# Moving the tanh of a feed-forward gate between the exps of attention's forward slots

## The chip, the cores and the metric

One core of a Trainium2 chip runs the whole program. The metric is the device time of one execution in microseconds (us); runs of one kernel agree within some tenths of a per cent. The engines have separate instruction queues, each worked off in order: PE (matrix multiplication; its weight loads are shown as PEld), DVE (vector), ACT (activations), POOL (GpSimd) and SP (issues most DMAs). They wait for each other by semaphores.

## What is computed

Forward and backward of a transformer block in parallel form, for one sequence of 2048 tokens of width 448, 16 heads of width 28, a feed-forward width of 1792:

```
xn  = layernorm(x)
out = x + attention(xn; wqkv, wo) + (silu(xn @ w_gate) * (xn @ w_up)) @ w_down
returned: out, and the gradients of x, wqkv, wo, w_gate, w_up, w_down for a given grad_out
```

Inputs and outputs are bf16. silu(a) is built from a tanh: with t = tanh(a / 2), silu(a) = a (1 + t) / 2, and the gradient of silu needs t too.

## The kernel before

The kernel has a forward stage and a backward stage, and the order of all instructions is written out by hand. The edit is in the forward stage.

**Slots.** Attention's scores and exponentials are cut into 256 slots: 4 groups of 4 heads, 4 chunks of 512 queries, 16 tiles of 128 keys. The function `slot(i)` issues, in this order:

- four score matmuls on PE (L625), one for each head, that run side by side in rows of 32. The first two write the tile `s_w`, which has one buffer of two PSUM banks; the other two write one bank each of `s_ps`, which has three buffers for two tiles in each slot. So the first two of a slot wait for the wide exp of the slot before, and the fourth waits for the first single exp of the slot before;
- three exps on ACT: a wide one over both banks of `s_w` (L628, 128x1024) and two single ones over the `s_ps` banks (L630, 128x512 each). They write `eT` tiles, which `o_unit` multiplies with the values (L467) once four slots are complete;
- filler work, by `fill.pump(FWD_NS, i)`. The class `Fillers` holds a list of units, written as generators that issue a matmul and yield its assumed cost in ns. In each slot it issues units until their costs reach a budget of 1740 ns. Attention's own later steps (`o_unit`, `mid1` to `mid3`, `dwo_unit`) are put first, and then a fixed stream, `items`.

**The stream.** For each of the 14 chunks of the feed-forward width (`fc`) and 4 token chunks (`sc`), 56 pairs in all, there are an `a_unit` (gate projection, L380), a `u_unit` (up projection, L404) and a `dh_unit` (gradient of the hidden layer, L418), two rounds apart: a round is a(i), then the gate work of i-1 with u(i-2), then dh(i-2). Between them stand weight-gradient units `dw_unit` (L437, 16 matmuls that read `f_sp`, the DMA transpose of a pair's results `hda`, issued on SP) and the qkv projections of the next head group (L292). Units take PSUM banks `gen` in turn.

**The tanh.** After its four matmuls an `a_unit` copies the result from PSUM with DVE (`ag`, L385) and issues the tanh on ACT (`tt`, L386), within the filler work of its slot; so on ACT's queue it stands behind the second single exp of that slot and ahead of the wide exp of the next one. `gate_ops` (L394 on DVE, L395 to L397 on POOL) reads `tt` and `ag` a round later, and `u_unit` and `dh_unit` read what it leaves (L410, L411, L423, L424). `tt` has two buffers, `ag` three.

The forward ends with the last slot and the end of the stream; `turn_loads` then issues the loads of the backward's first operands on SP (L742 to L747). The backward (from L763 on) is not touched.

Of the kernel before, what the change touches and what calls it, by code (L numbers as in the profile page):

```python
# [8 lines left out]
ACT = mybir.ActivationFunctionType  # L9
# [96 lines left out]
def kernel(  # L106
# [23 lines left out]
    PE, DVE, ACTE, POOL, SP = nc.tensor, nc.vector, nc.scalar, nc.gpsimd, nc.sync  # L130
# [63 lines left out]
    def new_gen(shape, dtype, name):  # L194
        return fill.bank().tile(shape, dtype, name=name)
# [156 lines left out]
    def load_fw(fc):  # L352
        w = ff.tile([P, 3, DP_], BF16, name="w_f")
        wT = ff.tile([P, 3, 4, P], BF16, name="wT_f", bufs=3)
        w4 = w[:].rearrange("p a (c f) -> p a c f", c=4)
        POOL.memset(w4[64:, 0:2, 3, :], 0.0)
        POOL.memset(w[:, 2, D:], 0.0)
        fsl = slice(fc * P, (fc + 1) * P)
        for a, src in ((0, B_w_gate), (1, B_w_up)):
            POOL.dma_start(out=w4[:, a, 0:3, :], in_=src[0:384, fsl].rearrange("(c p) f -> p c f", p=P))  # L360
            POOL.dma_start(out=w4[:64, a, 3, :], in_=src[384:448, fsl])
        POOL.dma_start(out=w[:, 2, :D], in_=B_w_down[fsl, :])
        fw[fc] = (w4[:, 0], w4[:, 1], wT[:, 2], lambda: sp_transpose(
            wT[:].rearrange("p a c d -> p (a c) d"), w[:].rearrange("p a n -> p (a n)"),
            (wT_d[:, fc], wT[:, 0:2].rearrange("p a c d -> p a (c d)"))))
        if fc > 0:
            fw_T(fc)
# [6 lines left out]
    def a_unit(fc, sc):  # L374
        if sc == 2 and fc + 1 < NFC:
            load_fw(fc + 1)
        ssl = slice(sc * 512, (sc + 1) * 512)
        ps = new_gen([P, 512], FP32, name="gen")
        for c in range(4):
            PE.matmul(ps[:], lhsT=fw[fc][0][:, c, :], rhs=xnT[:, c, ssl], start=(c == 0), stop=(c == 3))  # L380
            if c < 3:
                yield 216
        ag = ff.tile([P, 512], FP32, name="ag", bufs=3)
        tt = ff.tile([P, 512], FP32, name="tt")
        DVE.tensor_copy(out=ag[:], in_=ps[:])  # L385
        ACTE.activation(out=tt[:], in_=ag[:], func=ACT.Tanh, scale=0.5)  # L386
        ffs[fc, sc] = [ag, tt]
        yield 216

    def gate_ops(fc, sc):  # L390

        ag, tt = ffs[fc, sc]
        nn = ff.tile([P, 512], FP32, name="nn")
        DVE.scalar_tensor_tensor(out=ag[:], in0=tt[:], scalar=1.0, in1=ag[:], op0=ALU.add, op1=ALU.mult)  # L394
        POOL.tensor_scalar(out=nn[:], in0=tt[:], scalar1=-0.5, scalar2=0.5, op0=ALU.mult, op1=ALU.add)  # L395
        POOL.tensor_tensor(out=nn[:], in0=nn[:], in1=ag[:], op=ALU.mult)  # L396
        POOL.tensor_tensor(out=nn[:], in0=nn[:], in1=tt[:], op=ALU.add)  # L397
        ffs[fc, sc].append(nn)
# [63 lines left out]
    def o_unit(g, qc, m, eTs):  # L462
        ps = new_gen([P, 512], FP32, name="gen")
        for kt in range(4 * m, 4 * m + 4):
            for hh in range(4):
                r = HP * pv(hh)
                PE.matmul(ps[r:r + HP, :], lhsT=VS[g][:, kt, r:r + HP], rhs=eTs[kt][hh // 2][:, hh % 2, :],  # L467
                          start=(kt % 4 == 0), stop=(kt % 4 == 3), tile_position=(0, r), skip_group_check=True)
            if kt % 4 < 3:
                yield 216  # L470
        if m == 0:
            oacc[g, qc] = wk.tile([P, 512], FP32, name="oacc")
            DVE.tensor_copy(out=oacc[g, qc][:], in_=ps[:])
        else:
            DVE.tensor_tensor(out=oacc[g, qc][:], in0=ps[:], in1=oacc[g, qc][:], op=ALU.add)
        o_done.add((g, qc, m))
        yield 316

    def mid1(g, qc):
        acc = oacc.pop((g, qc))  # L480
        ps = new_gen([P, 4, P], FP32, name="gen")
        for qi in range(4):
            PE.transpose(ps[:, qi, :], acc[:, qi * P:(qi + 1) * P], ident_f[:])
            if qi < 3:
                yield 260
        o4 = ps[:].rearrange("p q (h r) -> p q h r", r=HP)
        rl = wk.tile([P, 4, 4], FP32, name="rl")
        DVE.reciprocal(out=rl[:], in_=o4[:, :, :, 28])
        t = wk.tile([P, 2, 4, P], BF16, name="od", bufs=5)
        DVE.tensor_tensor(out=t[:, 0].rearrange("p q (h r) -> p (q h) r", r=HP),  # L490
                          in0=ps[:].rearrange("p q (h r) -> p (q h) r", r=HP),
                          in1=rl[:].rearrange("p q h -> p (q h)").unsqueeze(2).to_broadcast([P, 16, HP]),
                          op=ALU.mult)
        od[g, qc] = (t, rl)
        yield 260

    def mid2(g, qc):
        t, rl = od[g, qc]
        ps = new_gen([P, 4, P], FP32, name="gen")
        for qi in range(4):  # L500
            for c in range(4):
                tok = (qc * 4 + qi) * P
                PE.matmul(ps[:, qi, :], lhsT=dyT[:, c, tok:tok + P], rhs=woT[:, c, g * P:(g + 1) * P],
                          start=(c == 0), stop=(c == 3))
                if qi * 4 + c < 15:
                    yield 60
        p3 = ps[:].rearrange("p q (h r) -> p (q h) r", r=HP)
        rl1 = rl[:].rearrange("p q h -> p (q h)")
        prod = wk.tile([P, 16, HP], FP32, name="prod", bufs=1)
        DVE.tensor_tensor(out=prod[:], in0=p3, in1=rl1.unsqueeze(2).to_broadcast([P, 16, HP]), op=ALU.mult)  # L510
        late_q.append((t, prod, rl1))
        yield 60
# [23 lines left out]
    def dwo_unit(g):  # L536
        ps = new_gen([P, 512], FP32, name="gen")
        for t in range(NT):
            PE.matmul(ps[:, :D], lhsT=od[g, t // 4][0][:, 0, t % 4, :], rhs=dy_sp[:, t, :],
                      start=(t == 0), stop=(t == NT - 1))  # L540
            if t < NT - 1:
                yield 189
        o = wk.tile([P, D], BF16, name="dw_o", bufs=1)
        DVE.tensor_copy(out=o[:], in_=ps[:, :D])  # L544
        for hh in range(4):
            h = g * 4 + hh
            (POOL if g == G - 1 else SP).dma_start(out=out_3[h * DH:(h + 1) * DH, :], in_=o[HP * pv(hh):HP * pv(hh) + DH, :])
        yield 189
# [10 lines left out]
    def ug(b, j):  # L559
        if j < len(chain):  # L560
            gate_ops(*chain[j])
        yield from u_unit(*b)
# [47 lines left out]
    def once(u):  # L610
        next(u)
        yield 0

    def slot(i):
        nonlocal eTs
        g, qc, kt = i // 64, (i // 16) % 4, i % 16
        qsl = slice(qc * 512, (qc + 1) * 512)
        m = i - EB // 2
        if m >= 0 and m % 4 == 0:
            fill.until(lambda: (m // 64, (m // 16) % 4, (m % 16) // 4) in o_done, i)  # L620
        wide = ps_w.tile([P, 2, 512], FP32, name="s_w")
        sp4 = [wide[:, 0], wide[:, 1]] + [ps_s.tile([P, 512], FP32, name="s_ps")[:] for _ in range(2)]
        for hh in range(4):
            r = HP * hh
            PE.matmul(sp4[hh], lhsT=KK[g][r:r + HP, kt * P:(kt + 1) * P], rhs=QQ[g][r:r + HP, qsl],  # L625
                      start=True, stop=True, tile_position=(r, 0))
        e2 = [wk.tile([P, 2, 512], BF16, name="eT", bufs=EB) for _ in range(2)]
        ACTE.activation(out=e2[0][:], in_=wide[:], func=ACT.Exp, scale=SCALE)  # L628
        for j in range(2):
            ACTE.activation(out=e2[1][:, j], in_=sp4[2 + j], func=ACT.Exp, scale=SCALE)  # L630
        eTs[kt] = e2
        if kt % 4 == 3:
            fill.first.append((i + 1, lambda e=dict(eTs): o_unit(g, qc, kt // 4, e)))
        if kt == 15:
            fill.first.append((i + 3, lambda: mid1(g, qc)))
            fill.first.append((i + 4, lambda: mid2(g, qc)))
            m3 = mid3(g, qc)
            fill.first.append((i + 5, lambda: once(m3)))
            fill.first.append((i + 6, lambda: once(m3)))
            fill.first.append((i + 7, lambda: once(m3)))  # L640
            if qc == 3:
                fill.first.append((i + 6, lambda: dwo_unit(g)))
            eTs = {}
        fill.pump(FWD_NS, i)
# [25 lines left out]
    for t in range(4):  # L670
        run(T_unit(xnT, xn_t, t, t % 2 == 0, ps_s if t < 2 else None))
    DVE.tensor_reduce(out=r_ones[:],
                      in_=ident_f[:].rearrange("p (a b) -> p a b", b=HP)[:, :, 28:30],
# [771 lines left out]
```

## Time and profile before

| | us |
|---|---|
| median of 3 runs | 1437.01 (1435.54 to 1440.87) |
| span of the profiled execution | 1438.2 |
| its forward slots with tanhs in them: scores of slot 14 to scores of the last slot | 53.3 to 608.1 |
| first backward score matmul | 616.3 |

The profiled execution has no time of its own beside its span, from the first instruction to the last; the span is 1.2 us over the median of the runs.

A row of a group of instructions reads: line of the kernel, engine, operation, tiles written <- tiles read, shapes, count | busy us, mean ns of one | idle us of the engine just before them, and which instruction ended that idle time. A row of the waits reads: who waited <- for whom: total us, times, longest. A row of the timeline reads: start, duration, engine, line, operation, and in brackets the idle time before it and what ended it. PEclk is the clock that PE was granted, as a share of full speed. Matmuls are pipelined and their ends are modelled, so PE's busy time can hold waits.

### The profile page before, as it was taken

The numbers are of one execution on the slowest core, as the hardware profiler recorded it, in microseconds if no ns is written. First come the engines' busy times: TensorE is split into PE (matmuls) and PEld (weight loads), VectorE is DVE, ScalarE is ACT, GpSimd is POOL, SyncE is SP. The second block draws the span as 40 slices with busy tenths as digits, with TensorE's granted clock in tenths as the row PEclk, the third lists the DMA queues.
The fourth block names the chain that finished last, engine by engine and source line by source line (L and its number), as shares of the span: only waits on it lengthen the run. The fifth ranks groups of instructions, "written<-read, shape, count | busy, mean of one in ns | idle before, by whom it ended". The sixth has DMA issues, their size and how long they took to land. (4 is left out here: it accounts for less than half of the span.)

```text
span 1438.2 us, 34638 instructions
## 1 busy us (share of the span) xinstructions
PE 1321.2 (92%) x12625; PEld 539.0 (37%) x12686; DVE 1154.8 (80%) x2001; ACT 1264.2 (88%) x2190; POOL 411.8 (29%) x577
## 2 busy tenths in 40 slices
PE   5899999989999999989999989999999999999995
PEld 2333333333333333333343434433443334443333
DVE  6677757656666676578999989888899999999988
ACT  4799988989889998869999989999989999899974
POOL 6574514454434454211121211201111112020005
PEclk9999999999999999989999999999999999999998
DMA  5796957796578676699999999999999999999981
GB/s 154 183 205 160 237 116 169 179 190 157 149 164 191 153 155 153 176 243 233 219 213 227 206 227 173 221 219 223 223 169 200 200 216 218 212 186 207 190 142 60
DMA packets 681116, 270.22 MB, mean 188 GB/s; under 512 B 607338, under 2 KB 655970, under 8 KB 680946
## 3 DMA queue, kind: packets, MB, share of 16 engines
q1 hardware_dynamic: 672498, 254.78, 87.1%
q0 software_dynamic: 7040, 12.93, 4.1%
q8 instruction: 99, 1.62, 0.5%
q14 instruction: 71, 0.58, 0.1%
q10 hardware_dynamic: 1408, 0.30, 0.1%
HBM read 64.37 MB, written 59.62 MB: 86 GB/s over the span
## 5 line engine op out<-in xcount | busy, mean ns | idle before, releaser
L864 DVE TENSOR_TENSOR ds_sb<-db,e_sb 128x512 bf16<-128x512 f32 x1024 | 646.5, 685 | 48.6 <-issue 22.4
L858 ACT ACTIVATE e_sb<-sb 128x512 bf16<-128x512 f32 x1024 | 555.0, 611 | 53.7 <-PE db L842 37.1
L628 ACT ACTIVATE eT<-s_w 128x1024 bf16<-128x1024 f32 x256 | 263.8, 1030 | 47.0 <-PE s_ps L625 43.8
L630 ACT ACTIVATE eT<-s_ps 128x512 bf16<-128x512 f32 x512 | 280.2, 611 | 0.0
L842 PE MATMUL db<-kd,qd 32*128 32x512 bf16 x1024 | 238.0, 385 | 8.6 <-DVE ds_sb L864 7.5
L834 PE MATMUL sb<-kd,qd 32*128 32x512 bf16 x1024 | 210.9, 389 | 5.3 <-DMA qd<-QD_d 3.4
L983 POOL TENSOR_TENSOR dq_acc<-dq_acc,dq_st 128x256 f32<-128x256 f32 x64 | 46.4, 724 | 497.7 <-ACT dq_st L981 497.7
L941 PE MATMUL acc<-ds_sb,qd 128*32 128x512 bf16 x1024 | 161.3, 391 | 0.0
L937 PE MATMUL acc<-e_sb,qd 128*32 128x512 bf16 x1024 | 159.2, 392 | 1.3 <-DVE dw_o L544 1.3
L924 ACT COPY dsT<-db 128x1024 bf16<-128x1024 bf16 x128 | 130.0, 1016 | 18.4 <-PE db L919 17.3
L396 POOL TENSOR_TENSOR nn<-nn,ag 128x512 f32<-128x512 f32 x56 | 71.3, 1274 | 249.7 <-DVE ag L394 241.1
L625 PE MATMUL s_ps<-QQ,KK 32*128 32x512 bf16 x512 | 126.2, 385 | 4.1
L1149 PE MATMUL genb<-wguT,dau_c 128*128 128x448 bf16 x448 | 117.5, 355 | 6.3 <-ACT dq_st L981 3.9
L625 PE MATMUL s_w<-QQ,KK 32*128 32x512 bf16 x512 | 100.2, 387 | 12.8 <-ACT eT L628 9.8
L834 PEld LDWEIGHTS <-qd 32*128 32x128 bf16 x1024 | 48.2, 91 | 146.3 <-issue 136.9
L437 PE MATMUL gen<-xn_t,f_sp 128*128 128x448 bf16 x416 | 91.8, 354 | 2.6 <-DVE nn L411 1.7
L437 PEld LDWEIGHTS <-f_sp 128*128 128x128 bf16 x640 | 55.7, 98 | 76.7 <-issue 31.6
L919 PE MATMUL db<-ident_bf,ds_sb 128*128 128x128 bf16 x1032 | 80.3, 222 | 0.9 <-DVE ds_sb L864 0.9
L968 PE MATMUL genb<-dsT,kd 128*32 128x256 bf16 x2048 | 79.2, 274 | 1.1
L919 PEld LDWEIGHTS <-ds_sb 128*128 128x128 bf16 x1032 | 69.1, 99 | 23.6 <-issue 5.1
L397 POOL TENSOR_TENSOR nn<-nn,tt 128x512 f32<-128x512 f32 x56 | 72.1, 1287 | 4.4
L625 PEld LDWEIGHTS <-KK 32*128 32x128 bf16 x1024 | 29.1, 91 | 115.3 <-issue 112.5
(179 smaller groups left out, 1951.7 us busy)
## 6 DMA issues: line engine op xcount, KB each, us to landing
F_d<-hda SPq DMA_DIRECT2D x56, 384.0 KB
dau_c<-F_d SPq DMA_DIRECT2D x24, 512.0 KB
qd<-QD_d SPq DMA_DIRECT2D x16, 512.0 KB
kd<-KD_d SPq DMA_DIRECT2D x16, 384.0 KB
dsT<-ds_sb SPq DMA_TRANSPOSE x383
h_c<-F_d SPq DMA_DIRECT2D x8, 512.0 KB
wT_d<-wT_f SPq DMA_DIRECT2D x14, 256.0 KB
KD_d<-qk_sp SPq DMA_DIRECT2D x7, 512.0 KB
```

The costliest lines, as they stand in the source:

```text
L437: PE.matmul(ps[:, :D], lhsT=fsp[fc][:, t // 4, w, t % 4, :], rhs=rhs[:, t, :], start=(t == 0), stop=(t == NT - 1))
L625: PE.matmul(sp4[hh], lhsT=KK[g][r:r + HP, kt * P:(kt + 1) * P], rhs=QQ[g][r:r + HP, qsl], start=True, stop=True, tile_position=(r, 0))
L628: ACTE.activation(out=e2[0][:], in_=wide[:], func=ACT.Exp, scale=SCALE)
L630: ACTE.activation(out=e2[1][:, j], in_=sp4[2 + j], func=ACT.Exp, scale=SCALE)
L834: PE.matmul(s_ps[:], lhsT=qside[g, qc][r:r + HP, 0, qi * P:(qi + 1) * P], rhs=kside[g, kc][r:r + HP, 0, :], start=True, stop=True, tile_po ...
L842: PE.matmul(d_ps[:], lhsT=qside[g, qc][r:r + HP, 1, qi * P:(qi + 1) * P], rhs=kside[g, kc][r:r + HP, 1, :], start=True, stop=True, tile_po ...
L858: ACTE.activation(out=est[k][:, j], in_=sps.pop((k, j))[:], func=ACT.Exp, scale=SCALE)
L864: DVE.tensor_tensor(out=ds[:, j], in0=dps.pop((k - 1, j))[:], in1=est[k - 1][:, j], op=ALU.mult)
L919: PE.transpose(ps[:, c, :], ds[:, c // 4, (c % 4) * P:(c % 4 + 1) * P], ident_bf[:])
L924: ACTE.copy(out=o, in_=ps[:])
L937: PE.matmul(a[r:r + HP, :], lhsT=sp4[:, 1, r:r + HP], rhs=e[:, j, :], start=first, stop=last, tile_position=(0, r), skip_group_check=True)
L941: PE.matmul(a[r:r + HP, :], lhsT=sp4[:, 0, r:r + HP], rhs=ds[:, j, :], start=first, stop=last, tile_position=(0, r), skip_group_check=True)
```

## The change

The `a_unit` no longer issues the tanh, but puts it on a list. `slot` issues what is on the list between its two single exps. `gate_ops` first issues its own pair's tanh, should that still be on the list.

```diff
@@ a_unit
         DVE.tensor_copy(out=ag[:], in_=ps[:])
-        ACTE.activation(out=tt[:], in_=ag[:], func=ACT.Tanh, scale=0.5)
+        tanhs.append((fc, sc, tt, ag))
         ffs[fc, sc] = [ag, tt]
         yield 216
 
+    tanhs = []
+
+    def tanh_flush(*only):
+        for x in list(tanhs):
+            if not only or x[:2] == only:
+                tanhs.remove(x)
+                ACTE.activation(out=x[2][:], in_=x[3][:], func=ACT.Tanh, scale=0.5)
+
     def gate_ops(fc, sc):
-
+        tanh_flush(fc, sc)
         ag, tt = ffs[fc, sc]
@@ slot
         for j in range(2):
             ACTE.activation(out=e2[1][:, j], in_=sp4[2 + j], func=ACT.Exp, scale=SCALE)
+            if j == 0:
+                tanh_flush()
         eTs[kt] = e2
```

On ACT's queue the order around a tanh was: single, single, **tanh**, wide, single, single. It becomes: single, single, wide, single, **tanh**, single.

## The prediction

> **What bounds the kernel now.** The edit touches one activation of the forward stage, so I read the page's engine rows, then the groups of ScalarE (ACT), the waits, and single slots of the timeline. The page (engine, busy us, share of the span, instructions):
>
> ```profile
> PE 1321.2 (92%) x12625; PEld 539.0 (37%) x12686; DVE 1154.8 (80%) x2001; ACT 1264.2 (88%) x2190; POOL 411.8 (29%) x577
> ```
>
> PE and ACT are both near full, but a mean over stages does not say who waits. The tanhs run from 54.1 to 578.7 us, within the forward slots (start of slot 14 at 53.3, last scores at 608.1). Groups of ACT, whole span (count | busy, mean ns | idle before, by whom):
>
> ```profile
> L628 ACT ACTIVATE eT<-s_w 128x1024 bf16<-128x1024 f32 x256 | 263.8, 1030 | 47.0 <-PE s_ps L625 43.8
> L386 ACT ACTIVATE tt<-ag 128x512 f32<-128x512 f32 x56 | 35.8, 640 | 18.5 <-DVE ag L385 13.2 <-POOL nn L397 2.3 <-DVE dl L525 1.4
> L340 ACT ACT_TABLE_LOAD x1 | 1.3, 1283 | 3.5 <-issue 3.5
> ```
>
> ACT has 47.0 us of idle time waiting for scores: in the forward it is mostly PE that sets the pace. But in 18.5 us it stands before a tanh whose input is not there, with the next wide exp queued behind it. Does PE pay for that? The waits between 56 and 611 us (total, times, longest):
>
> ```profile
> ACT eT L628 <- PE s_ps L625: 32.2, 71, 3.9
> ...
> ACT tt L386 <- DVE ag L385: 12.5, 22, 1.5
> ...
> PE s_w L625 <- ACT eT L628: 9.8, 20, 2.3
> ```
>
> PE waits 9.8 us openly. The timeline of slot 122 (start, us, ..., idle before) shows that this is not all:
>
> ```profile
> 300.50 0.39 PE L625 MATMUL s_w<-QQ,KK 32*128 32x512 bf16 x2
> ...
> 300.73 0.68 DVE L385 COPY ag<-gen 128x512 f32<-128x512 f32 x1
> ...
> 301.51 0.63 ACT L386 ACTIVATE tt<-ag 128x512 f32<-128x512 f32 x1 [0.82 <-DVE ag L385]
> ...
> 302.05 1.01 ACT L628 ACTIVATE eT<-s_w 128x1024 bf16<-128x1024 f32 x1
> ...
> 302.95 1.08 ACT L630 ACTIVATE eT<-s_ps 128x512 bf16<-128x512 f32 x2
> ...
> 303.10 0.39 PE L625 MATMUL s_w<-QQ,KK 32*128 32x512 bf16 x2 [0.40 <-ACT eT L628]
> ...
> 303.11 0.85 PE L625 MATMUL s_ps<-QQ,KK 32*128 32x512 bf16 x2
> ```
>
> In an undisturbed slot the wide exp starts 0.49 us after the scores; here 302.05 - 300.50 = 1.55, as the tanh waited for its copy until 301.51. The next scores then wait 0.40 us for the one wide bank. Their last two matmuls take 0.85 instead of 0.39: the fourth, in the third s_ps bank, waits another 0.46 us for the first single exp, and all later PE work with it. That counts as busy. So this slot lost 0.40 + 0.46 = 0.86 us of PE.
>
> **The change part by part.** It removes and adds no instruction, DMA or buffer. 56 tanhs of 0.64 us move past one wide and one single exp of the next slot on ACT's queue; nothing moves on SP's or POOL's. Two slots of 56 may differ: the gate work of the first pairs comes so soon that it flushes its tanh itself.
>
> Step 1, the waits before the tanh go. In its new place a tanh starts at the earliest 0.49 + 0.90 + 0.48 = 1.87 us after its slot's scores (exp starts 0.90 apart after a wide one, 0.48 after a single one). Its copy is done by 1.63 us at the latest in every slot (the trace's copy ends against the scores), so it waits no more; only the third tanh has another wait, POOL's until 59.1 us, and there the wide exp has passed before it. The ceiling is the 18.5 us.
>
> Step 2, what of that reaches PE. Slot 122 again: wide at 300.99, single 301.89, tanh 302.37, last single 302.91, ACT free at 303.39. Scores of slot 123 come at 302.70 without a wait; their wide exp would start at 303.19 and starts at 303.39, 0.20 late; its first single ends at 303.39 + 0.90 + 0.61 = 304.90 and lets the fourth matmul of slot 124 go at 304.95. PE fills 2.11 us between, so slot 124 starts at 304.81, and that matmul is 0.14 late. Lost: 0.14 in place of 0.86. I did the same sum for all slots from 14 to 255, with the filler time of PE as it ran, a wide exp 1.00 + 0.05 before the next scores, a single one 0.61 + 0.05 before the fourth matmul, and 0.54 us of ACT for a tanh. For the order of before it puts the last scores at 607.6 (read: 608.05), with 38.3 us lost on PE behind ACT; for the new order 21.7; without any tanh 14.6. So tanhs cost 23.7 us of PE now and 7.1 after: **-16.6 us**, all of it from the 31 tanhs with over 60 ns of idle before them. Moving the 25 others alone comes to +0.6 or nothing: a ready tanh delays the next wide exp as much from one place as from the other.
>
> Step 3, what is late next. PE also waits for DVE and DMA in the forward, some 19 us. Where DVE is behind (nine places, waits of 0.2 to 1.3 us), PE gets there earlier and waits longer, by at most what was gained since DVE last stood idle. Summed over them that gives **+3.2 us**.
>
> Step 4, what comes later than before. Behind the tanh now stands the second single exp, 0.54 us later. Its readers are the o units' last matmuls, and only in slots whose index is 3 mod 4, some 14 tanhs. Such an exp then ends about 3.0 us after its scores, the matmul comes 2.16 + 1.0 after them: covered by 0.1 on the median, short by as much in quick slots. Bounds 0 and 14 x 0.2 = 2.8; I take **+1.0**, near the median. The gate work L394 (DVE) and L395 (POOL) reads the tanh: from the trace, tanh ends in the new place come before their starts in all but the first two slots, by 0.23 us at the least; no cost, or 0.5 us of DVE each if those few slip, and DVE has 33% idle time there.
>
> A rule speaks against putting a tanh among exps. The Trainium skill ("ScalarE: Activation LUTs", "Table sets: the hidden batching unit") says to batch by table set, and prices a switch at 2.66 us. Its table has exp and tanh in one set, so the rule gives 0; were they in two, 56 tanhs with two switches each would be an estimated 298 us. The trace decides: one table load in the whole span, with 56 alternations already.
>
> Sum: -16.6 + 3.2 + 1.0 = -12.4 us. The profiled span is 1438.2, 1.2 above the runs' median of 1437.0; I take the difference from the median: **1424.6**. The backward stage starts when the forward's last units are through: the loads of its first operands are issued at 611.5 behind stores that follow PE's last copies, so its 820 us shift along.
>
> **The rivals.** (A) The forecast, bounded by 1437.0 - 18.5 = 1418.5 and, with steps 3 and 4 doubled, 1428.8.
>
> (B) Only the open waits are worth something: if the late fourth matmul holds up nothing, 9.8 us is all there is, and 9.8 - 3.2 - 1.0 = 5.6 gives 1431.4. For it: PE's waits show just that. Against: after each long pair (303.11 + 0.85) the filler starts at 303.89, not at 303.43.
>
> (C) Slower: the weight-gradient units (L437) overtake the transposes of f_sp. Thirteen of fourteen found them landed, the least 5.75 us after issue; one did not:
>
> ```profile
> PE gen L437 <- DMA f_sp<-hda: 3.7, 1, 3.7
> ```
>
> ```profile
> 312.00:314.00 2.00, 1.78 (x6) 0.76 (x8) 0.62 (x1) 1.92 (x3) 0.00 (x0) 0.59 0.51 154
> 314.00:316.00 2.00, 2.00 (x9) 0.43 (x8) 1.29 (x2) 0.71 (x2) 0.00 (x0) 0.56 1.10 242
> ```
>
> (Second view: stretch, its length, busy of PE, PEld, DVE, ACT, POOL, granted clock, DMA share, GB/s.) The granted clock after it is 0.59 and 0.56 for 4 us, another 1.7 us, so 5.4 each. To be 7.2 us slower, four more of them are needed: (12.4 + 7.2) / 5.4 = 3.6. With four: 1437.0 - 12.4 + 21.6 = 1446.2. Against: the transposes are issued behind DVE's work on PE's results and so come earlier too; between issue and use little is gained.
>
> (D) Nothing comes of it: gates flush nearly every tanh where it stood, or the gain ends at the turn to the backward, where PE waits 3.4 us for the qd load. 1437.0. Against: in 54 of 56 cases the gate starts 2.8 us or more after the scores of the next slot.
>
> **How the numbers follow.** A measurement of this kernel can tell about 0.5%, 7.2 us, from no change: faster is under 1429.8. A 0.72, B 0.14, D 0.05, C 0.09; so faster 0.72, same 0.14 + 0.05 = 0.19, slower 0.09. The range goes from A's ceiling, 1418.5, past B to 1431.5; it leaves out C, D and a little of A.
>
> **What would show it.** ACT's idle before L386 falls from 18.5 to under 3, and the wait of PE's s_w for ACT from 9.8 to 2 to 4 us; L625's second pair at 0.85 becomes rarer but stays after short slots; last scores near 596 in place of 608; the stretch from there to the end unchanged within 2 us. It is wrong if those waits fall and the last scores do not move (B or D), or if L437 waits for f_sp more than once or twice (C).

## The result, and the profile after

The changed kernel takes 1431.7 us (median of 7 runs, 1428.6 to 1433.7) against 1440.2 of the kernel before (7 runs, among them the three from which the prediction took its base); the ratio is 0.9946 (95% interval 0.9928 to 0.9965). Two more sessions with the same program gave 0.9938 (0.9918 to 0.9958) and 0.9948 (0.9927 to 0.9968). Over all of these it is 1431.8 us (19 runs) against 1440.3 (38 runs): 8.5 us faster. Forecast were 12.4, and 1424.6 as the time; 1431.7 lies 0.2 above the range.

Line numbers have moved on by 8 to 10: the scores are L633, the exps L636 and L638, the tanh L396. In the groups of ACT (count | busy, mean ns | idle before, by whom) the idle time before the tanh is gone, and it stands before the wide exp now, that is, ACT waits for PE:

```profile
L636 ACT ACTIVATE eT<-s_w 128x1024 bf16<-128x1024 f32 x256 | 264.5, 1033 | 54.3 <-PE s_ps L633 52.1
...
L396 ACT ACTIVATE tt<-ag 128x512 f32<-128x512 f32 x56 | 35.5, 634 | 2.5 <-POOL nn L405 1.9 <-DVE ag L385 0.6
```

The open wait of PE's scores for ACT, 9.8 us before, is 1.2 in the page's groups:

```profile
L633 PE MATMUL s_w<-QQ,KK 32*128 32x512 bf16 x512 | 100.1, 387 | 3.7 <-ACT eT L636 1.2
```

Slot 122, the example of the prediction, in the timeline of the changed kernel:

```profile
298.76 0.39 PE L633 MATMUL s_w<-QQ,KK 32*128 32x512 bf16 x2
...
299.25 1.02 ACT L636 ACTIVATE eT<-s_w 128x1024 bf16<-128x1024 f32 x1
...
300.17 0.59 ACT L638 ACTIVATE eT<-s_ps 128x512 bf16<-128x512 f32 x1
...
300.65 0.63 ACT L396 ACTIVATE tt<-ag 128x512 f32<-128x512 f32 x1
...
300.90 0.39 PE L633 MATMUL s_ps<-QQ,KK 32*128 32x512 bf16 x2
...
301.64 1.04 ACT L636 ACTIVATE eT<-s_w 128x1024 bf16<-128x1024 f32 x1
...
303.04 0.55 PE L633 MATMUL s_ps<-QQ,KK 32*128 32x512 bf16 x2
```

The wide exp starts 0.49 us after the scores and the tanh waits for nothing. The scores of slot 123 are not held up (0.39), and the fourth of slot 124 is late by 0.55 - 0.39 = 0.16 us, by the starts 0.18; the sum had 0.14. Before, this slot had cost 0.86.

What PE waits for in the changed forward (56 to 611 us; total, times, longest) shows what has come instead:

```profile
PE gen L445 <- DMA f_sp<-hda: 4.1, 2, 3.0
...
PE gen L445 <- DVE nn L419: 2.7, 6, 1.1
PE gen L511 <- DVE nn L419: 2.2, 2, 1.4
PE gen L475 <- ACT eT L638: 2.2, 1, 2.2
...
PE gen L412 <- DVE hda L432: 1.8, 4, 1.1
```

Three profiled executions of either kernel size the steps. "Waits for scores" is the idle time of PE before a slot's first score matmul, where ACT ended it, and the lateness of the fourth against the first, by their starts and beyond the usual 0.01 us, over slots 14 to 255; the others are PE's waits in the same stretch.

| us | before, three executions | mean | changed, three executions | mean | difference | forecast |
|---|---|---|---|---|---|---|
| waits for scores | 38.8, 38.2, 37.8 | 38.3 | 21.7, 21.5, 21.3 | 21.5 | -16.8 | -16.6 |
| for DVE | 15.3, 15.1, 15.1 | 15.2 | 19.2, 18.2, 18.5 | 18.6 | +3.4 | +3.2 |
| o units for exps | 0.6, 0.6, 0.6 | 0.6 | 2.8, 2.8, 2.8 | 2.8 | +2.2 | +1.0 |
| for f_sp | 3.7, 2.2, 3.8 | 3.2 | 4.1, 4.3, 5.5 | 4.6 | +1.4 | 0 |
| last forward scores at | 608.1, 604.8, 609.6 | 607.5 | 597.1, 599.3, 598.6 | 598.3 | -9.2 | -12.4 |
| from there to the end | 830.1, 832.7, 831.6 | 831.5 | 834.6, 829.5, 832.1 | 832.1 | +0.6 | 0 |

The four waits add up to -9.8, the forward is 9.2 us shorter in the mean, and the span 8.6. The three executions of either kernel did not have the same clock; what that does to the 9.2 stands under "The loss that was none".

### The profile page after: what moved, and what is told of

Same layout as the page of the kernel before. It is cut to its first block, busy times and chain, and to the rows that moved or that the text cites. A ratio compares the mean times of both kernels' runs of the same rounds, so it can differ in the third digit from the quotient of the medians.

```text
span 1431.7 us, 34641 instructions
## 1 busy us (share of the span) xinstructions
PE 1322.1 (92%) x12625; PEld 542.0 (38%) x12686; DVE 1153.3 (81%) x2001; ACT 1263.1 (88%) x2190; POOL 411.6 (29%) x577
## 5 line engine op out<-in xcount | busy, mean ns | idle before, releaser
L636 ACT ACTIVATE eT<-s_w 128x1024 bf16<-128x1024 f32 x256 | 264.5, 1033 | 54.3 <-PE s_ps L633 52.1
L638 ACT ACTIVATE eT<-s_ps 128x512 bf16<-128x512 f32 x512 | 287.2, 614 | 0.0
L633 PE MATMUL s_ps<-QQ,KK 32*128 32x512 bf16 x512 | 119.8, 385 | 2.3
L633 PE MATMUL s_w<-QQ,KK 32*128 32x512 bf16 x512 | 100.1, 387 | 3.7 <-ACT eT L636 1.2
L405 POOL TENSOR_TENSOR nn<-nn,tt 128x512 f32<-128x512 f32 x56 | 72.8, 1299 | 4.4
L475 PE MATMUL gen<-eT,VS 128*32 128x512 bf16 x1024 | 68.3, 382 | 5.7 <-ACT eT L638 2.2
```

## The experiments

**Two executions more of the changed kernel.** The first pair of profiles had lost 4.5 us between the forward's end and the end of the span. Was that the change's doing?

> The changed kernel once more, unaltered. Theory 1: the edit saves 17 us of PE's waits for scores, 6 us come back in the forward as waits for DVE and for late exps, and the forward ends 11.0 us earlier in every execution; the 4.5 us that the profiled pair lost after that are half-clock windows that fall elsewhere in each execution. So here the last forward scores come near 597 again, and the time from there to the end, 830.1 before and 834.6 after, lies anywhere between 827 and 836. Theory 2: the backward's opening is made slower by the earlier start, each time; then it is 834 or more again. Ratio to the kernel before 0.993 to 0.996 either way.

> The changed kernel a third time, unaltered, to size the whole. If the gain of the forward is the 11 us of the first pair at equal clock, less what half-clock windows take in one execution or another, the last forward scores come between 596 and 600, PE's waits for scores are 21 to 22 us, and the time from there to the end is 829 to 835. Ratio to the kernel before 0.993 to 0.995: 7 to 10 us.

Measured: last forward scores at 599.3 and 598.6, from there to the end 829.5 and 832.1. The 4.5 us are not in every execution; theory 2 expected 834 or more in each.

**The kernel before, twice more.**

> The kernel before once more, unaltered. Theory 1 (half-clock windows fall elsewhere in each execution): the waits for scores are 38 to 39 us again and the last forward scores come within 2 us of 608, but the time from there to the end is not 830.1 again; on the mean of the two new executions of this kernel it is 832 to 834, as in the changed kernel (834.6, 829.5). Theory 2 (the earlier start makes the backward slower): it stays at 830 or below in both.

> The kernel before a third time, unaltered; both theories expect of it what they expect of the second execution, and the two are taken together.

Measured: waits for scores 38.2 and 37.8, last scores at 604.8 and 609.6 (the first beyond the 2 us expected), from there to the end 832.7 and 831.6, mean 832.2. Theory 2 needed 830 or less. The two kernels do not differ in the backward by anything that these executions show.

**The tanh between the wide exp and the first single one.** This tells whether the late fourth matmul, which PE's waits hardly show, costs time.

```diff
+        tanh_flush()
         for j in range(2):
             ACTE.activation(out=e2[1][:, j], in_=sp4[2 + j], func=ACT.Exp, scale=SCALE)
-            if j == 0:
-                tanh_flush()
```

> The tanh goes between the wide exp and the first single exp of the next slot. Theory 1 (the fourth score matmul waits for the first single exp, and all of PE with it, though that counts as busy): the open wait of PE's first scores for ACT stays near 1 us, but the fourth matmul comes later; the slot sum gives 38.8 us lost behind ACT, as much as before the change (38.3), so the forward ends near 608 again and the ratio is 0.998 to 1.002. Rival B of the prediction (only the open waits cost time): as the changed kernel, forward end near 597, ratio 0.994.

Measured: ratio 0.9996 (0.9980 to 1.0011), last scores at 607.2, waits for scores 39.8. The tanh waits no more here either (2.6 us in all), and the open wait of a slot's first scores is 0.7. Two rows of PE's waits, and a slot near 299 us in the timeline:

```profile
PE s_ps L633 <- ACT eT L639: 8.1, 14, 2.4
...
PE s_w L633 <- ACT eT L636: 0.7, 4, 0.2
```

```profile
299.43 1.02 ACT L636 ACTIVATE eT<-s_w 128x1024 bf16<-128x1024 f32 x1 [0.38 <-PE s_ps L633]
300.35 0.62 ACT L396 ACTIVATE tt<-ag 128x512 f32<-128x512 f32 x1
300.87 1.08 ACT L639 ACTIVATE eT<-s_ps 128x512 bf16<-128x512 f32 x2
...
301.01 0.88 PE L633 MATMUL s_ps<-QQ,KK 32*128 32x512 bf16 x2
```

A tanh there is 0.52 us of delay for the first single exp, and the fourth matmul of the next slot stands 0.88 - 0.39 = 0.49 us late with PE behind it. So removing the tanh's own wait is worth nothing if the tanh then stands ahead of the exp that PE waits for. Rival B is refuted: it expected the changed kernel's time.

**Which tanhs.** The 31 that had idle time before them were moved alone, then the 25 others alone (by a list of indices, `LATE`):

```diff
         tanhs.append((fc, sc, tt, ag))
+        if not (4 * fc + sc in LATE):
+            tanh_flush(fc, sc)
```

> Only the 31 tanhs that had over 60 ns of idle time before them are moved; the other 25 stay at the end of their unit. Step 2 of the prediction: all of the saving is theirs, so PE's waits for scores (open ones and late fourth matmuls) are 21.7 us, as in the changed kernel, and the last forward scores come at 596 to 599. Rival: a tanh that is ready costs less in the new place too; then the waits are 25 us or more.

> Only the other 25 tanhs are moved. Step 2: nothing is saved; the waits for scores are 38 to 40 us and the last forward scores come at 607 to 609. Rival: 35 us or less and 605 or earlier.

Measured, the 31 alone: waits for scores 21.5 us, last scores at 597.8; the 25 alone: 35.6 and 607.0. These are one execution each (1429.5 and 1441.3 us, beside 1438.5 for the kernel before), so the waits say more than the times. All of the change in the waits comes with the 31. With the 25 alone 2.7 us of waits went too, where the sum had +0.6; these 2.7 do not add to the others, as the changed kernel, with all 56 moved, has 21.5 as well.

**The tanh behind the second single exp of the next slot**, so in its old place in the order, but one slot later (`j == 1` in the flush). And the same in every fourth slot alone, the one that an o unit follows (`j == (kt % 4 == 3)`):

> The tanh goes behind the second single exp of the next slot, so it is on the same place of the order as before, one slot later. Theory 1: what counts is that its input is there, not the place; PE's waits for scores stay at 21 us (21.7 in the changed kernel), and the wait of the o units' matmuls for the second single exp falls from 2.7 us to the 0.4 of before; the forward ends 2 us before that of the changed kernel, ratio to the kernel before 0.991 to 0.995. Rival: the place between the singles matters, because the wide exp is delayed by a ready tanh; then the waits for scores rise by up to 25 x 0.25 = 6 us and the forward ends 4 to 6 us later than that of the changed kernel.

> The changed kernel, but in slots whose index is 3 mod 4, which an o unit follows, the tanh goes behind the second single exp. If step 4 was too small because the o units wait for that exp, their wait falls from 2.7 us to under 1 with nothing else changed, and the forward ends 1 to 2 us before the changed kernel's 597 to 599. Rival: DVE takes it back, as it took 2.8 of the 2.4 to 2.7 us that moving all tanhs behind the second single exp saved; then the forward ends as in the changed kernel.

Measured: waits for scores 21.4 and 20.2, so the place between the singles is not what counts. The o units' waits fell from 2.8 to 0.6 in both; but PE's waits for DVE rose from 18.6 to 21.4 and 21.5, so last scores came at 596.0 and 596.8, and the ratios, 0.9940 (0.9916 to 0.9964) and 0.9956 (0.9941 to 0.9971), are those of the changed kernel. That fits the rival of the second run: what the o units gave, DVE took. The forward ends of these two single executions do not decide it; the changed kernel's first execution, with the same 3.4 us at half clock, has 597.1, so they are 1.1 and 0.3 us earlier, where 2 and 1 to 2 were expected. Most of the exchange is at a single place, near 61 us. In the changed kernel (first ACT, then PE, from the timelines by engine):

```profile
57.36 0.66 ACT L396 ACTIVATE tt<-ag 128x512 f32<-128x512 f32 x1
59.90 0.63 ACT L396 ACTIVATE tt<-ag 128x512 f32<-128x512 f32 x1 [1.88 <-POOL nn L405]
60.44 0.58 ACT L638 ACTIVATE eT<-s_ps 128x512 bf16<-128x512 f32 x1
```

```profile
57.86 1.04 PE L475 MATMUL gen<-eT,VS 128*32 128x512 bf16 x15
61.06 0.38 PE L475 MATMUL gen<-eT,VS 128*32 128x512 bf16 x1 [2.17 <-ACT eT L638]
61.37 0.68 PE L336 MATMUL gen<-ident_bf,dy_t 128*128 128x128 bf16 x5
```

The third tanh needs the buffer that POOL reads for the first pair until 59.9. The second single exp of slot 15 stands behind it, and the sixteenth matmul of the o unit waits 2.17 us for that exp. With the tanh behind the exp the o unit goes through, and the transposes after it wait instead, for DVE's step L419 on the first pair. With the tanh behind the exp in every slot this wait is 2.23 us, and L419 had itself waited for POOL's L405, the last reader of that buffer. In the version for every fourth slot the transposes start at 61.7 us:

```profile
PE gen L336 <- DVE nn L419: 2.4, 1, 2.4
```

**No tanh at all**, a bound for any place:

```diff
-        ACTE.activation(out=tt[:], in_=ag[:], func=ACT.Tanh, scale=0.5)
+        tt = tt_c        # one tile, set to zero once
```

> No tanh at all: the gate work reads one constant tile of zeros instead, so the 56 tanhs are left out and nothing else. Bound for any place of the tanh. Theory 1: the slot sum gives 14.6 us of PE lost behind ACT, 7 less than in the changed kernel; with a third of that given back to DVE the forward ends 4 to 6 us before the changed kernel's 597, near 592. Rival (DVE and DMA already pace the changed forward): no earlier than 596.

Measured: waits for scores 14.6 us, to the tenth what the sum gave. Last scores at 592.8. PE's waits for DVE are 23.4: of the 6.9 us that the changed kernel could still lose at the scores, 4.8 come back as waits for DVE. The ratio is 0.9923 (0.9895 to 0.9952). So this one execution leaves 598.3 - 592.8 = 5.5 us in the forward for any other place of the tanh; as it had 10.2 us at half clock, against 6.8 in the mean of the changed kernel's three, a bound of some 7 us is the safer reading (an estimate: 3.4 us more at half clock cost at most 1.7).

**The first gate step on POOL**, to see whether it is DVE's load that gives the time back:

```diff
-        DVE.scalar_tensor_tensor(out=ag[:], in0=tt[:], scalar=1.0, in1=ag[:], op0=ALU.add, op1=ALU.mult)
+        POOL.tensor_scalar(out=nn[:], in0=tt[:], scalar1=1.0, scalar2=1.0, op0=ALU.mult, op1=ALU.add)
+        POOL.tensor_tensor(out=ag[:], in0=nn[:], in1=ag[:], op=ALU.mult)
```

> The changed kernel with the first step of the gate, (1 + tanh) times the projection, on POOL (one tensor_scalar and one tensor_tensor, 1.9 us) and no more on DVE (0.7 us). If PE's waits behind DVE are a matter of DVE's load (step 3), they fall from 17.7 us to 12 or less and the forward ends 3 to 5 us before that of the changed kernel, ratio to the kernel before 0.990 to 0.993. Rival: those waits are bursts of single units that 40 us less work spread over the stage does not shorten, or POOL's longer chain becomes late; then the forward ends no earlier, ratio 0.994 or more.

> Tanhs behind the second single exp of the next slot, and the first step of the gate on POOL. If both steps hold, what the o units no longer wait for is not taken back by DVE: the forward ends 2 us before that of the kernel with the gate step on POOL alone, ratio to the kernel before 0.988 to 0.992. Rival: as that one, or later, because the gate comes right behind its tanh and POOL's chain is late for the up unit.

Measured: PE's waits for DVE 18.3 and 20.7 us, in place of the 12 expected; last scores at 601.4 and 599.5; ratios 0.9965 (0.9950 to 0.9981) and 0.9951 (0.9930 to 0.9973). The 56 steps that left DVE had taken 39.0 us, and DVE's busy time fell by 24.5 us in the first version (from 1153.3 to 1128.8); PE's waits for it did not get shorter. Whether they are bursts of single units or POOL's longer chain handed on through DVE, these two runs do not separate in full. POOL's chain is part of it: in the first version DVE's step that reads POOL's result (L420) waited 7.4 us for POOL, against 1.7 in the changed kernel, and the wait near 61 us grew from 2.2 to 3.4 us, at the o unit in the first version and at the transposes in the second. The waits on `hda` fell meanwhile, in the first from 7.0, 6.2 and 7.0 to 3.2. The last scores of these two executions came after 17.1 us at half clock each, against 3.4 to 10.2 in the changed kernel's, and the granted clock in all seven runs of the first version was 0.974 to 0.976, against 0.978 in the mean of the changed kernel's 19; so their times cannot be laid to POOL alone. Why the clock was lower there stays open. No version beats the changed kernel by more than the intervals.

## Why the prediction was right or wrong

**The mechanism was right, and its main term held.** Step 1: the tanh's idle time fell from 18.5 to 2.5 us (under 3 was forecast). The open wait of `s_w` fell further than forecast, to 1.2 us instead of 2 to 4. Step 2: -16.8 against -16.6, and the sum for slots hit the waits of four other orders as well: 21.7 as expected and 21.5 measured for the 31 alone, 38.8 and 39.8 behind the wide exp, 14.6 and 14.6 without tanhs, 21 and 21.4 behind the second exp. It failed on the 25 alone (38 to 40 against 35.6). Rivals B and D are out: the experiment behind the wide exp has B's condition and not its time, and all 56 tanhs did move. That B's 1431.4 lies nearer to the measured 1431.7 than the forecast of 1424.6 is chance: it is a gain of 5.6 us, too small, taken from a base that was too low.

**Step 3**, what DVE takes back, was right in sum, +3.2 against +3.4; its nine places were not compared one by one.

**The step that failed is step 4: too small, and in the wrong place.** It spread 1.0 us over 14 quick slots. It measured 2.2 us, at one place. The prediction had seen the third tanh's wait for POOL in step 1 and let it go, "there the wide exp has passed before it"; what had not passed is the second single exp, and the o unit behind it. Nor is that wait a new one. In the kernel before, the same tanh held the wide exp of slot 15, and with it the scores of slot 16 (first ACT, then PE):

```profile
59.14 0.63 ACT L386 ACTIVATE tt<-ag 128x512 f32<-128x512 f32 x1 [1.96 <-POOL nn L397]
59.68 1.01 ACT L628 ACTIVATE eT<-s_w 128x1024 bf16<-128x1024 f32 x1
```

```profile
60.74 0.39 PE L625 MATMUL s_w<-QQ,KK 32*128 32x512 bf16 x2 [2.30 <-ACT eT L628]
```

The 2.30 us that PE waited here, the longest of its open waits, are in the saving of step 2; they came back as the 2.17 us of the o unit, and with the tanh behind the second exp as the 2.23 and 2.41 us of the transposes. What stands behind it is POOL's work on the first pair: with the gate step added to it, the wait is 3.4 us. None of the places tried removed it; it passed from one reader to the next. A wait that is moved has to be followed to every instruction behind it, not just to the one that mattered before.

**Rival C came in part**, 1.4 us of it, and the sum had it at 0. The unit that the prediction named as the nearest, 5.75 us from issue to use, is the one that now waits: 1.1, 1.3 and 1.3 us near 229 us in the three executions, against 0 to 0.2 before. The four long stalls that would have made it slower did not come; the one old stall is 3.0, 3.0 and 4.1 us, against 3.7, 2.0 and 3.6.

**The remainder and the base.** Taken as waits that add up, of the 12.4 - 8.5 = 3.9 us that were missing, 1.2 are step 4, 1.4 f_sp, 0.2 step 3, less 0.2 of step 2. The other 1.3 stand as 0.6 in the forward, 0.6 after it, and 0.1 between spans and runs; they are within what executions of one program differ by. The sum had no term for the granted clock either. Over the runs it was 0.9783 in the mean for the changed kernel (19 runs) and 0.9796 for the kernel before (34 that list it), and within either kernel a run whose clock is 0.001 lower is on average 0.6 to 1.1 us longer; by that some 1 us of the missing 3.9 goes with the clock (an estimate). Whether the change lowers it stays open. The time itself was missed by 7.1 us, and 3.3 of these, the largest single share, are the base: three runs had given 1437.0, and 38, those three included, gave 1440.3. A gain of 12.4 from there would be 1427.9, within the range.

**The loss that was none.** The first pair of profiles alone says 11.0 us gained in the forward and 4.5 lost behind it, and a story for that was at hand: an earlier start meeting older DMA work. The granted clock from 600 to 730 us (last columns: clock, DMA share, GB/s; before, then changed) seems to support it:

```profile
600.00:730.00 130.00, 116.84 (x1211) 48.44 (x1208) 103.86 (x172) 108.26 (x197) 18.00 (x30) 0.92 1.05 223
```

```profile
600.00:730.00 130.00, 116.73 (x1197) 48.41 (x1197) 107.69 (x179) 104.58 (x192) 21.72 (x36) 0.88 1.09 222
```

But the changed kernel's second and third executions have 0.92 in the same stretch, and two others of the kernel before 0.91 and 0.92. In the trace the clock falls to one half for stretches of 3.41 us or a small multiple. In the forward these lie mostly near 60 to 75 and near 310 us, but not in each execution; added up (us; "forward" is from slot 14 to the last scores):

| execution | half clock in the forward | last scores at | half clock after them | from there to the end |
|---|---|---|---|---|
| before, 1st | 3.4 | 608.1 | 37.0 | 830.1 |
| before, 2nd | 0.0 | 604.8 | 50.2 | 832.7 |
| before, 3rd | 6.8 | 609.6 | 41.7 | 831.6 |
| changed, 1st | 3.4 | 597.1 | 57.0 | 834.6 |
| changed, 2nd | 10.2 | 599.3 | 33.6 | 829.5 |
| changed, 3rd | 6.8 | 598.6 | 43.5 | 832.1 |

After the last scores, the more time at half clock, the longer the rest, in the same order for all six and whichever the kernel. In the forward the same holds within either kernel, and at equal time at half clock (3.4, and 6.8) the changed kernel is some 11 us earlier; the 9.2 us of the means has 3.4 us more of half clock on the changed side. So the 4.5 us of the first pair go with the clock. The lengths are in line with the Trainium skill ("TensorE: Matmul & The Clock Gate", "What's actually happening"), which has a gate that judges PE by windows of some 3.4 us that run on by themselves and do not start with the kernel. That the stretches are the whole of the scatter is not shown: the kernel without tanhs took 839.0 us after its last scores, 4.4 more than any other. It had the most time at half clock there too, 60.6 us, but only 3.6 more than the changed kernel's first execution, and what the rest is stays open.

## What to carry to other kernels

An instruction on an in-order queue costs what it makes the next one wait, so put it where its input is already there and behind, not ahead of, the instruction that the pacing engine waits for; here the same tanh, one exp earlier, was worth nothing. Look for such waits in the start times of the pacing engine's instructions, as a group of concurrent matmuls hides them in its busy time. Then follow every wait that remains to all that stands behind it in its new place: a wait that has another cause than the place goes along, and size a gain of half a per cent by several executions on each side, not by one pair.

## What the runs showed of the hardware that was not expected

- One program's forward stage ended at 604.8, 608.1 and 609.6 us in three executions, with the same 38 us of waits for scores in each and 0.0, 3.4 and 6.8 us at half clock. A single profile is worth some 3 us in 600 here; two profiles with the same time at half clock compare better.
- PE's busy share of the span is 92% in the first profile of either kernel, though the forward ends 11 us earlier in the second. The Trainium skill ("Perfetto Trace Analysis", "Identifying the Most-Contended Engine") says that matmul busy time is a poor measure of PE's headroom. Its reason is that pipelined instructions look smaller; here a row of two matmuls of 0.85 us with 0.46 us of waiting in it shows a way in which they look larger.
